# Blocks 2 to 5 take the product with w_in by quarters, with partial sums kept in one PSUM bank per pair of tiles

## The chip, the cores and the metric

One Trainium2 chip, one of its cores. The metric is the device time in microseconds (us) of one execution of the whole program. The kernel before took 990.42 us (median of three executions, 988.54 to 991.31).

## The reference

```python
for t in range(S):                                   # 4 batches, 8 heads, S = 768, head_dim 64
    state = gamma * state + k[t] (x) v[t]
    y[t]  = scale * q[t] @ state
x   = y as (3072, 512)
xn  = x / rms(x) * rms_g
x2  = (silu(xn @ w_gate) * (xn @ w_val)) @ w_out     # d_ff 1536
h   = x2 @ w_in                                      # 512 -> 1024
e   = exp(h - max(h)); solu = h * e / (sum(e) + 1e-9)
out = layernorm(solu) * g_ln @ w_out2                # 1024 -> 512
```

Everything is float32.

## The kernel before

The 3072 tokens are six blocks of 512 (`NB = 6`), each of four tiles of 128. A block goes through two stages. The first (`bc_block`, or `seven_block` for block 5) makes x2, transposed, in the four PSUM banks X0 to X3 (`XB`, a bank for 128 of the 512 features): twelve steps `m`, each with the gate product in bank GB, the value product in VB (`gv`) and their product with a slice of `w_out` (`cmm`). The second (`de_block`) takes x2 from the X banks, multiplies by `w_in`, makes softmax and layer norm, transposes and multiplies by `w_out2`. Banks SB and YB serve the attention part of the next block, which runs beside the first stage.

Every matmul of full precision is three fp32r matmuls: each operand is split into a high part (ScalarE's copy, L98) and a low part (a subtraction on VectorE or GpSimd, L99), and `mm3` (L723 to 726) multiplies high by high, high by low and low by high. `seven_block` already does the gate and value products with seven products of quarters in place of eight, with sums of the weights that `sums_steps` makes in blocks 2 to 4 and stores in DRAM.

In `de_block`, `x2_split` splits the four X banks; `d_mm(n, t, s)` makes h for tile t in two banks (`HB`): 4 slices of features x 2 halves of `w_in` x 3 matmuls, 512 columns each, and then the softmax: two maxima (L928), two exponentials (L931), two products with h (L936), and the mean taken off, one half on VectorE and one on GpSimd (L941). `t_tr(t)` transposes the result on TensorE (L951) and splits it; `e_mm(n, t, s)` multiplies by `w_out2` into one bank and sends the result out (L989, L990).

The order is d0 d1 t0 d2 t1 e0 d3 t2 e1 t3 e2 e3. Work of the next block hangs on numbered slots, called as the stages go on: `w_load` (weights from DRAM, L653, on SP's queue into the four `w4` and two `wo` buffers), the steps of the norm (`rms_steps`) and the split of the next block's normalised input into `xnh` and `xnl`. The program order gives priorities; a planner at build time orders each engine's list by them and by the times that it expects, and `issue_after` ties an instruction behind another on its engine. On the chip each engine takes its list in order.

Of the kernel before, what the change touches and what calls it, by code (L numbers as in the profile page):

```python
# [33 lines left out]
CHAIN = 12  # L34
W2_AT = [36 + 2 * j for j in range(16)]
SEVEN = (5,)
SUMS_AT = [(n, s) for n in (2, 3, 4) for s in ((3, 10, 17, 24) if n == 2 else (1, 8, 15, 22))]


@with_exitstack  # L40
def retention_moe_kernel(ctx: ExitStack, tc: tile.TileContext, qk0, q2, kt, kv, wpk, w2i, w2o,
# [512 lines left out]
    def sums_steps(j, part):  # L554
# [32 lines left out]

        return [load, none, whole, sums, none, none, parts, none, store]

    def load64(key):  # L590
# [56 lines left out]
    def w_load(g, part):  # L647
        m = g % NM
        if g < NM:
            load64((m, part))  # L650
        elif g < NG:
            w = wtile(part)
            nc.sync.dma_start(w.bitcast(F32), scr[m][part])  # L653
            wsp[g, part] = w

    def w_conv(g, part):
# [207 lines left out]
    def seven_block(n):  # L864
        base = n * NM
        for j in range(NM // 2):
# [44 lines left out]
    def d_mm(n, t, s):  # L911
# [4 lines left out]
        for i, (k, hf) in enumerate(order):  # L916
            cs = slice(hf * 512, hf * 512 + 512)
            mm3(H[hf], x2h[k][:, ts_], x2l[k][:, ts_], w2["h"][:, k, cs], w2["l"][:, k, cs],
                k == 0, k == NK - 1)
            if i == 3:  # L920
                slot(n, s)
        V = nc.vector
# [3 lines left out]
        e, u = f4(), f4()  # L926
        for hf in range(2):
            V.tensor_reduce(out=mx[:, hf:hf + 1], in_=H[hf], axis=AX.X, op=ALU.max)  # L928
        V.tensor_reduce(out=nmx, in_=mx, axis=AX.X, op=ALU.max, negate=True)
        for hf in range(2):  # L930
            nc.scalar.activation(e[:, hf, :], H[hf], AF.Exp, bias=nmx, accum_out=se[:, hf:hf + 1])  # L931
        if t == NCB - 1 and n not in (1, NB - 1) and PRE & 1:

            nc.scalar.activation(sm[:, 11:12], se[:, 1:2], AF.Silu)
        for hf in range(2):
            V.scalar_tensor_tensor(out=u[:, hf, :], in0=H[hf], scalar=1.0, in1=e[:, hf, :],  # L936
                                   op0=ALU.mult, op1=ALU.mult, accum_out=su[:, hf:hf + 1])
        V.tensor_tensor(out=mu, in0=su[:, 0:1], in1=su[:, 1:2], op=ALU.add)
        V.tensor_scalar(mu, mu, 1.0 / D_FF2, None, ALU.mult)  # L939
        for hf, eng in ((0, V), (1, nc.gpsimd)):  # L940
            eng.tensor_scalar(u[:, hf, :], u[:, hf, :], mu, None, ALU.subtract)  # L941
        lnst[t] = (u, sm)
        slot(n, s + 1)

    def t_tr(t):

        u, sm = lnst[t]
        res = []
        for b in range(2):
            bank = HB[t][b]  # L950
# [14 lines left out]
        G.tensor_tensor(out=w, in0=w, in1=r, op=ALU.mult)  # L965
        lnst[t] = (res, w)

    def e_mm(n, t, s):
        res, w = lnst.pop(t)
        r0 = n * 512 + t * P  # L970
        if n == NB - 1 and t == NCB - 1 and TAIL:

            for B, hs in ((EB[t], slice(0, 256)), (EB[0], slice(256, 512))):
# [8 lines left out]
        for f in range(NF):  # L982
            hi, lo = res[f // 4]
            cs = slice((f % 4) * P, (f % 4) * P + P)
            mm3(EB[t], hi[:, cs], lo[:, cs], w2["oh"][:, f, :], w2["ol"][:, f, :], f == 0, f == NF - 1)
            if f == 3:
                slot(n, s)
        o = f4()[:, 0, :]
        nc.scalar.mul(o, EB[t], w)  # L989
        nc.scalar.dma_start(out[r0:r0 + P, :], o)  # L990
        slot(n, s + 1)

# [15 lines left out]
    def x2_load():  # L1008
        srcs = []
        for d in range(NK):  # L1010
            t = st()
            nc.sync.dma_start(t, x2scr[d])
            srcs.append(t)
        return srcs

    def de_block(n, srcs, base):

# [130 lines left out]
    for n in range(NB):  # L1148
        if n + 1 < NB:
# [2 lines left out]
            elif n == 1:  # L1152
                begin, span, r = 35, 21, (57, 58, 59, 59, 60, 60, 61, 62, 63, 64)
            else:
                begin, span, r = 0, 28, (30, 31, 32, 32, 33, 33, 36, 38, 40, 42)
            pieces = att_pieces(n + 1)
            for i, f in enumerate(pieces):
                extra.setdefault((n, begin + i * span // (len(pieces) - 1)), []).append(f)
            if n + 1 in SEVEN:
                r = (30, 31, 32, 32, 33, 33, 36, 37, 38, 39, 40, 41, 42, 43, 44, 45, 46)  # L1160
                first7 = [lambda: seven_load(n + 1)] \
                    + [lambda i=i: w_load((n + 1) * NM + i, 2) for i in range(2)] + [seven_pump]
                for s, f in zip((37, 38, 38, 45), first7):
# [87 lines left out]
```

## Time and profile before

| | us |
|---|---|
| median of three executions | 990.42 |
| profiled execution | 990.47 |
| its span | 988.7 |
| TensorE (PE) busy | 976.0 (99%) |
| VectorE (DVE) busy | 462.8 (47%) |
| GpSimd (POOL) busy | 422.2 (43%) |
| ScalarE (ACT) busy | 395.5 (40%) |

The span runs from the first to the last instruction; what lies around it, 1.8 us, is part of the time. Busy time of TensorE includes matmuls that overlap the next one, so the distance between starts has to be read from the timeline. HBM reads were 172.05 MB and writes 38.80 MB.

### The profile page before, as it was taken

Reading aid. Unit: us, or ns where it says so; the run is one execution under the profiler, and the core shown is the slowest. Engines: PE = TensorE matmul, PEld = TensorE weight load, DVE = VectorE, ACT = ScalarE, POOL = GpSimd, SP = SyncE. Lnnn points to the kernel's source line nnn. Section 1 sums busy time; section 2 is a strip of 40 time slices with the busy share of each in tenths; the row PEclk is TensorE's granted clock in tenths of the full one; section 3 lists DMA queues with packets and bytes.
Section 4 is the critical chain, followed back from the end, with each engine's and each line's share of the span. In section 5 each row is a group of like instructions: output and inputs, shape, how many; then the busy total and the mean of one; then the engine's idle time right before and its main releaser. Section 6 shows DMA issues by size and latency. Waiting matters only on the chain.

```text
span 988.7 us, 15957 instructions
## 1 busy us (share of the span) xinstructions
PE 976.0 (99%) x5916; PEld 813.7 (82%) x5916; DVE 462.8 (47%) x920; ACT 395.5 (40%) x768; POOL 422.2 (43%) x517
## 2 busy tenths in 40 slices
PE   8999999999999999999999999999999999999998
PEld 7878787888888887888888888788888888999887
DVE  4787784662464743234462224463323353443552
ACT  4766664582344442222443123344212344221333
POOL 6876873671142593253543223655032372000031
PEclk9799999999999999999999999999999999999999
DMA  9699999887512135898523889723597724697200
GB/s 351 238 333 403 334 315 379 328 303 243 172 53 87 44 120 180 291 324 278 172 75 104 288 282 295 232 66 107 174 342 269 264 81 150 204 311 262 75 12 32
DMA packets 91021, 211.90 MB, mean 214 GB/s; under 512 B 10432, under 2 KB 36416, under 8 KB 90944
## 3 DMA queue, kind: packets, MB, share of 16 engines
q1 hardware_dynamic: 82160, 185.71, 56.1%
q10 hardware_dynamic: 8784, 25.17, 6.6%
q8 instruction: 47, 0.77, 0.3%
q14 instruction: 30, 0.25, 0.1%
HBM read 172.05 MB, written 38.80 MB: 213 GB/s over the span
## 4 chain that ended last, share of the span: by engine, by line
PE 87%; DMA 5%; POOL 3%; ACT 1%; DVE 1%; issue 1%; SPq 1%; ACTq 0%; POOLq 0%; DVEq 0%
PE X L724 12%; PE X L726 12%; PE X L725 12%; PE GB L724 7%; PE GB L726 7%; PE GB L725 7%; PE VB L724 6%; PE VB L726 6%; PE VB L725 6%; PE SB L117 3%; PE YB L117 2%; PE VB L834 2%; PE YB L834 2%; DMA x<-in_wpk 2%; PE SB L834 1%; PE GB L834 1%
## 5 line engine op out<-in xcount | busy, mean ns | idle before, releaser
L743 DVE TENSOR_TENSOR f<-VB,f 128x512 f32<-128x512 f32 x60 | 41.4, 690 | 153.6 <-PE VB L726 146.3
L725 PE MATMUL X<-r,wo 128*128 128x512 f32 x264 | 103.4, 392 | 0.0
L726 PE MATMUL X<-r,wo 128*128 128x512 f32 x264 | 103.0, 390 | 0.0
L724 PE MATMUL X<-r,wo 128*128 128x512 f32 x264 | 101.3, 394 | 0.7 <-DMA wo<-scr 0.7
L98 ACT CAST r<-f 128x512 fp32r<-128x512 f32 x72 | 44.5, 619 | 125.6 <-DVE f L743 107.8
L772 ACT ACTIVATE f<-GB 128x512 f32<-128x512 f32 x60 | 35.7, 594 | 147.7 <-PE GB L726 145.0
L625 POOL TENSOR_TENSOR st<-st,x 128x512 int32<-128x512 int32 x52 | 69.7, 1344 | 49.4 <-DVE st L624 11.3
L724 PE MATMUL GB<-xnh,w 128*128 128x512 f32 (+1 forms) x220 | 86.6, 394 | 1.7 <-ACT xnh L98 0.8
L724 PE MATMUL VB<-xnh,w 128*128 128x512 f32 (+1 forms) x220 | 86.0, 391 | 0.0
L725 PE MATMUL GB<-xnl,w 128*128 128x512 f32 (+1 forms) x220 | 85.6, 389 | 0.3 <-DVE xnl L99 0.2
L726 PE MATMUL VB<-xnh,w 128*128 128x512 f32 (+1 forms) x220 | 85.6, 389 | 0.0
L725 PE MATMUL VB<-xnl,w 128*128 128x512 f32 (+1 forms) x220 | 85.5, 388 | 0.0
L726 PE MATMUL GB<-xnh,w 128*128 128x512 f32 (+1 forms) x220 | 85.4, 388 | 0.0
L99 DVE TENSOR_TENSOR r<-f,r 128x512 fp32r<-128x512 f32 x72 | 60.4, 840 | 31.5 <-ACT r L98 31.0
L565 POOL TENSOR_TENSOR x<-x 128x512 f32<-128x512 f32 x24 | 31.0, 1292 | 98.2 <-DMA x<-scr 78.6
L961 POOL TENSOR_TENSOR sm<-sm 128x1 f32<-128x1 f32 x24 | 5.1, 214 | 134.2 <-DVE sm L939 114.7
L724 PEld LDWEIGHTS X<-r,wo 128*128 128x128 f32 x264 | 49.5, 188 | 11.4 <-issue 1.1
L726 PEld LDWEIGHTS X<-r,wo 128*128 128x128 f32 x264 | 49.6, 188 | 10.3
L725 PEld LDWEIGHTS X<-r,wo 128*128 128x128 f32 x264 | 49.6, 188 | 10.1 <-issue 0.2
L724 PE MATMUL X<-w2oh,r 128*128 128x512 f32 (+1 forms) x144 | 56.6, 393 | 0.0
L726 PE MATMUL X<-w2oh,r 128*128 128x512 f32 (+1 forms) x144 | 55.7, 387 | 0.0
L725 PE MATMUL X<-w2ol,r 128*128 128x512 f32 (+1 forms) x144 | 55.3, 384 | 0.0
(367 smaller groups left out, 2419.0 us busy)
## 6 DMA issues: line engine op xcount, KB each, us to landing
w<-scr SPq DMA_DIRECT2D x96, 512.0 KB, 4.7
wo<-scr SPq DMA_DIRECT2D x60, 512.0 KB, 4.4
x<-in_wpk SPq DMA_DIRECT2D x36, 512.0 KB, 6.2
x<-scr SPq DMA_DIRECT2D x24, 512.0 KB, 5.7
sscr<-x SPq DMA_DIRECT2D x24, 512.0 KB, 7.5
scr<-CV ACTq DMA_DIRECT2D x18, 512.0 KB, 6.1
rv<-in_kv SPq DMA_DIRECT2D x24, 256.0 KB, 4.7
scr<-w ACTq DMA_DIRECT2D x12, 512.0 KB, 5.6
```

Of the source, the lines that this page charges most:

```text
L98: h = nc.scalar.copy(hi, src)
L99: (lo_eng or nc.vector).tensor_tensor(out=lo, in0=src, in1=hi.bitcast(F32), op=ALU.subtract)
L117: return lambda: nc.tensor.matmul(out, lhsT=lhsT, rhs=rhs, start=start, stop=stop)
L565: nc.gpsimd.tensor_tensor(out=w[:, 0, :], in0=w[:, 0, :], in1=w[:, 1, :], op=ALU.add)
L625: nc.gpsimd.tensor_tensor(out=ti, in0=ti, in1=lo, op=ALU.add)
L724: nc.tensor.matmul(ps, lhsT=lh, rhs=rh, start=start, stop=False)
L725: nc.tensor.matmul(ps, lhsT=lh, rhs=rl, start=False, stop=False)
L726: return nc.tensor.matmul(ps, lhsT=ll, rhs=rh, start=False, stop=stop)
L743: recent["dve"] = nc.vector.tensor_tensor(out=a, in0=GV[1], in1=silu[:, 0, :], op=ALU.mult)
L772: recent["act"] = nc.scalar.activation(s[:, 0, :], GV[0], AF.Silu)
L834: nc.tensor.matmul(ps, lhsT=x, rhs=y[:, k, :], start=start and k + i == 0, stop=k == 1 and i == 2, skip_group_check=True)
L961: G.tensor_tensor(out=w, in0=r, in1=r, op=ALU.mult)
```

## The change

In blocks 2 to 5 `de_quarters` takes the place of `de_block`. x2 of the block is taken as quarters (tokens 0-255 and 256-511 by features 0-255 and 256-511) and `w_in` as quarters (features by halves of its 1024 columns). Seven products of quarters (`p1` to `p7`, each of two token tiles, 6 matmuls a tile) give h, with sums S1 to S4 of quarters of x2 made on VectorE and sums T1 to T4 of quarters of `w_in`. The latter are made once, in block 2 (`w2_sums`); T4 replaces a quarter of `w_in` in SBUF, T1, T2 and T3 go to DRAM and are loaded in every block, T1 into two `w4` buffers, T2 and T3 over `xnh` and `xnl`. P1, P6, P7 and, for a tile of the second pair, P4 are added up in one bank (GB for tiles 0 and 2, VB for 1 and 3); between them ScalarE copies the bank out (`keep`), and VectorE adds what P2, P5 and P3 left in X banks (`add`).

Since `xnh` and `xnl` are taken, the next block's split comes later (slots 46 to 49 in place of 36 to 42), and so do the sums of block 5's input; the first weights of blocks 3 and 4 are loaded at slots 39, 47 and 48. The sums for `seven_block` are made in two steps in block 2 and five each in blocks 3 and 4, where it was four in each. `soft` is the softmax of `d_mm`, with its tiles as arguments.

```diff
-SUMS_AT = [(n, s) for n in (2, 3, 4) for s in ((3, 10, 17, 24) if n == 2 else (1, 8, 15, 22))]
+SUMS_AT = [(2, 17), (2, 24)] + [(n, 1 + 6 * i) for n in (3, 4) for i in range(5)]
+W2_SUMS_AT = (2, 9)
+FIRST7 = 2
...
+    def w2_sums(k):
+        def whole():
+            for r in (k, k + 2):
+                W.append(wt("x2", [P, 2, 512], F32, 4))
+                nc.gpsimd.tensor_tensor(out=W[-1].rearrange("p a x -> p (a x)"), in0=w2["h"].bitcast(F32)[:, r, :],
+                                        in1=w2["l"].bitcast(F32)[:, r, :], op=ALU.add)
+        def sums():
+            (b11, b12), (b21, b22) = ((w[:, 0, :], w[:, 1, :]) for w in W)
+            for out, a, b in ((b11, b12, b11), (b12, b22, b12), (b22, b22, b11), (b21, b21, b22)):
+                nc.gpsimd.tensor_tensor(out=out, in0=a, in1=b, op=ALU.subtract)
...
-                elif g // NM not in SEVEN:
+                elif g // NM not in SEVEN and (part == 2 or g % NM > 1 or g // NM <= FIRST7):
...
@@ in bc_block @@
+        if n >= FIRST7:
+            t_load(1, n), t_load(2, n)
         cmm(n * NM + NM - 1, NM - 1)
...
@@ in seven_block @@
+        t_load(0, n)
+        with tc.issue_after(recent["wo"].ins):
+            t_load(1, n), t_load(2, n)
         out(NM - 2)
         out(NM - 1)
...
+    def t_load(i, n):
+        if i:
+            nc.sync.dma_start((None, xnh, xnl)[i].bitcast(F32), t2scr[i].rearrange("p a k x -> p (a k) x"))
+            return
+        T1[:] = [wt("w4", [P, 2, 512], F32R, 4) for _ in range(2)]
+        for a in range(2):
+            nc.sync.dma_start(T1[a].bitcast(F32), t2scr[0][:, a])
+
+    def de_quarters(n, base):
+        a11 = wt("x2", [P, 2, 2, 256], F32R, 4)
+        xh, xl = (wt("x2", [P, 2, 512], F32R, 4) for _ in range(2))
+        s3, s1, s2 = two(st()), two(st()), two(st())
+        for k in range(2):
+            split(a11[:, 0, k, :], a11[:, 1, k, :], XB[k][:, lo])
+            S.copy(s1[:, k, :], XB[k][:, hi])
+        for k in range(2):
+            V.tensor_tensor(out=s3[:, k, :], in0=XB[k][:, lo], in1=s1[:, k, :], op=ALU.subtract)
+        for k in range(2):
+            split(xh[:, k, :], xl[:, k, :], XB[2 + k])
+        for k in range(2):
+            i = V.tensor_tensor(out=s2[:, k, :], in0=XB[2 + k][:, hi], in1=s3[:, k, :], op=ALU.subtract)
+        S2 = two(r2()), two(r2())
+        s2h = S.copy(S2[0], s2)
+        s2l = V.tensor_tensor(out=S2[1], in0=s2, in1=S2[0].bitcast(F32), op=ALU.subtract)
+        S3 = parts(s3, nc.gpsimd)
...
+        def mul(bank, t, A, B, start=False):
+            ts_ = slice(t * P, t * P + P)
+            for k in range(2):
+                for i, (x, y) in enumerate(((A[0], B[0]), (A[0], B[1]), (A[1], B[0]))):
+                    nc.tensor.matmul(bank, lhsT=x[:, k, ts_], rhs=y[:, k, :], start=start and k + i == 0,
+                                     stop=k == 1 and i == 2, skip_group_check=True)
+        def keep(out, bank):
+            with tc.high_priority():
+                last["act"] = S.copy(out, bank)
+        def add(out, bank, q):
+            with tc.high_priority():
+                last["dve"] = V.tensor_tensor(out=out, in0=bank, in1=q, op=ALU.add)
...
+        def p1(t, Z):
+            mul(Z, t, A11, B11, True)
+            u[t] = f4()
+            keep(u[t][:, 0, :], Z), step()
+        def p2(t, Y):
+            mul(Y, t, A12, B21, True), add(u[t][:, 0, :], Y, u[t][:, 0, :]), step()
+        def p6(t, Z):
+            mul(Z, t, S2, T2), keep(u[t][:, 1, :], Z), step()
+        def p7(t, Z, tile):
+            mul(Z, t, S3, T3)
+            u[2 + t] = tile
+            keep(tile[:, 1, :], Z), step()
+        def p5(t, W):
+            mul(W, t, S1, (T1[0], T1[1]), True), step()
+        def c22(t, W):
+            add(u[2 + t][:, 1, :], W, u[2 + t][:, 1, :])
+        def p4(t, Z):
+            mul(Z, t, A22, T4), step()
+        def p3(t, W):
+            mul(W, t, S4, B22), add(u[t][:, 1, :], W, u[t][:, 1, :]), step()
+        p1(0, GB)
+        with tc.issue_after(s2h.ins):
+            p1(1, VB)
+        with tc.issue_after(s2l.ins):
+            p2(0, X0)
+        p6(0, GB)
+        p5(0, X1)
+        p7(0, GB, f4())
+        c22(0, X1)
+        p6(1, VB)
+        p4(0, GB)
+        soft(n, 2, (GB, u[2][:, 1, :]), halves(e2()), u[2], False)
+        p3(0, X1)
+        p7(1, VB, e2())
+        p5(1, X3)
+        with tc.issue_after(recent["sub"].ins):
+            c22(1, X3)
+        with tc.issue_after(last["act"].ins), tc.issue_after(last["dve"].ins):
+            soft(n, 0, (u[0][:, 0, :], u[0][:, 1, :]), (st(), st()), u[0], False)
+        p2(1, X2)
+        t_tr(2, (X0, X1))
+        p4(1, VB)
+        soft(n, 3, (VB, u[3][:, 1, :]), halves(e2()), u[3], False)
+        p3(1, X3)
+        soft(n, 1, (u[1][:, 0, :], u[1][:, 1, :]), halves(e2()), u[1], True)
+        t_tr(0, (X0, X1))
+        e_mm(n, 2, base + 15, GB)
+        t_tr(3, (X0, X1))
+        e_mm(n, 0, base + 17, X2)
+        t_tr(1, (X0, X1))
+        e_mm(n, 3, base + 19, X3)
+        e_mm(n, 1, base + 21, X2, True)
...
-        de_block(n, XB, 35)
+        if n >= FIRST7:
+            de_quarters(n, 35)
+            continue
+        de_block(n, XB, 35)
```

## Rows read from the trace of the kernel before

**Rows 1.** The page: busy us, share of the span, instructions of each engine.
```profile
PE 976.0 (99%) x5916; PEld 813.7 (82%) x5916; DVE 462.8 (47%) x920; ACT 395.5 (40%) x768; POOL 422.2 (43%) x517
```

**Rows 2.** Windows of stages: busy us of each engine, granted clock, DMA share, GB/s.
```profile
385.00:481.00 96.00, 96.00 (x621) 78.73 (x618) 32.48 (x58) 28.19 (x56) 41.15 (x48) 1.00 0.84 281
481.00:537.00 56.00, 56.00 (x352) 45.67 (x352) 26.36 (x69) 23.28 (x52) 25.51 (x44) 1.00 0.28 89
...
841.00:937.40 96.40, 95.73 (x651) 88.53 (x650) 40.86 (x94) 24.02 (x46) 1.15 (x4) 1.00 0.67 219
```

**Rows 3.** Waits of TensorE: us in total, times, longest us.
```profile
PE GB L724 <- ACT xnh L98: 0.8, 1, 0.8
...
PE X L724 <- DMA wo<-scr: 0.7, 1, 0.7
```

**Rows 4.** Tile x, TensorE's instructions: duration ns min/median/max, first and last start.
```profile
L724 PE MATMUL X<-w2ih,x x120: 389/389/496, 269.4 to 966.1; 128*128 128x512 f32 x120
...
L724 PE MATMUL VB<-w2ih,x x48: 389/389/497, 262.1 to 963.4; 128*128 128x512 f32 x48
```

**Rows 5.** TensorE's timeline in block 2: start us, duration us, instruction.
```profile
474.57 0.39 PE L726 MATMUL VB<-xnh,w 128*128 128x512 f32 x1
...
481.29 0.39 PE L724 MATMUL GB<-w2ih,x 128*128 128x512 f32 x1
...
489.29 0.39 PE L724 MATMUL X<-w2ih,x 128*128 128x512 f32 x1
...
494.50 0.39 PE L726 MATMUL X<-w2ih,x 128*128 128x512 f32 x1
...
508.20 0.39 PE L726 MATMUL GB<-w2oh,r 128*128 128x512 f32 x1
...
513.64 0.40 PE L726 MATMUL X<-w2ih,x 128*128 128x512 f32 x1
```

**Rows 6.** ScalarE's timeline in block 2, idle time before in brackets.
```profile
479.44 2.64 ACT L98 CAST x<-X 128x512 fp32r<-128x512 f32 x4 [0.94 <-PE X L726]
...
508.71 0.69 ACT L989 ACTIVATE f<-GB,sm 128x512 f32<-128x512 f32 x1 [2.71 <-PE GB L726]
```

**Rows 7.** VectorE's timeline in block 2.
```profile
480.48 2.48 DVE L99 TENSOR_TENSOR x<-X,x 128x512 fp32r<-128x512 f32 x4
...
488.81 0.69 DVE L928 TENSOR_REDUCE sm<-GB 128x1 f32<-128x512 f32 x1
...
493.60 0.49 DVE L941 TENSOR_SCALAR f<-f,sm 128x512 f32<-128x512 f32 x1
```

**Rows 8.** GpSimd's timeline in block 2.
```profile
493.70 1.83 POOL L941 TENSOR_SCALAR f<-f,sm 128x512 f32<-128x512 f32 x1
...
521.86 1.56 POOL L941 TENSOR_SCALAR f<-f,sm 128x512 f32<-128x512 f32 x1
```

**Rows 9.** Lines L743 (page: busy, mean ns), L772 and L860 (min/median/max).
```profile
L743 DVE TENSOR_TENSOR f<-VB,f 128x512 f32<-128x512 f32 x60 | 41.4, 690 | 153.6 <-PE VB L726 146.3
...
L772 ACT ACTIVATE f<-GB x60: 573/597/600, 42.4 to 788.9; 128x512 f32<-128x512 f32 x60
...
L860 DVE TENSOR_TENSOR f<-VB,st x6: 424/425/425, 852.7 to 926.4; 128x256 f32<-128x256 f32 x6
```

**Rows 10.** DMA issues: KB each, median us from issue to landing.
```profile
w<-scr SPq DMA_DIRECT2D x96, 512.0 KB, 4.7
```

**Rows 11.** GpSimd's timeline, sums of block 5's input, first and last of 11.
```profile
793.57 3.80 POOL L99 TENSOR_TENSOR xnl<-xT,xnh 128x512 fp32r<-128x512 f32 x3 [0.73 <-ACT xnh L98]
...
806.19 1.30 POOL L99 TENSOR_TENSOR qd<-xT,qd 128x512 fp32r<-128x512 f32 x1
```

**Rows 12.** TensorE's timeline in block 5, first and last of the stretch.
```profile
937.42 0.39 PE L724 MATMUL GB<-w2ih,x 128*128 128x512 f32 x1
...
985.05 0.28 PE L726 MATMUL GB<-w2oh,r 128*128 128x256 f32 x1
```

**Rows 13.** Window in the start-up, columns as in rows 2.
```profile
30.00:45.00 15.00, 14.00 (x97) 12.58 (x97) 11.91 (x16) 9.97 (x18) 14.46 (x18) 0.66 0.56 190
```

More of the change, by code (lines that the diff above doesn't have):

```diff
@@ L588, in sums_steps, with tied, parts, parts2 @@
         return [load, none, whole, sums, none, none, parts, none, store]
+    t2scr = [dp.tile([P, 2, 2, 512], F32, tag=f"t2scr{i}", name=f"t2scr{i}") for i in range(3)]
+    def w2_sums(k):
+        W, o = [], []
+        def whole():
[7 more added lines that the diff above has]
+                nc.gpsimd.tensor_tensor(out=out, in0=a, in1=b, op=ALU.subtract)
+        def tied(hi, lo, t):
+            with tc.issue_after(recent["act"].ins), tc.issue_after(recent["dve"].ins):
+                split(hi, lo, t)
+        def parts():
+            for t in (W[0][:, 0, :], W[1][:, 1, :]):
+                o.append(wt("x2", [P, 2, 512], F32R, 4))
+                tied(o[-1][:, 0, :], o[-1][:, 1, :], t)
+        def parts2():
+            tied(w2["h"][:, k, 512:], w2["l"][:, k, 512:], W[1][:, 0, :])
+            h, l = (wt("st", [P, 512], F32R, 3) for _ in range(2))
+            tied(h, l, W[0][:, 1, :])
+            o.extend((h, l))
+        def store():
+            for i in range(2):
+                nc.sync.dma_start(t2scr[i][:, :, k, :], o[i].bitcast(F32))
+        def store2():
+            for i in range(2):
+                nc.sync.dma_start(t2scr[2][:, i, k, :], o[2 + i].bitcast(F32))
+        def none():
+            pass
+        return [whole, none, sums, none, parts, parts2, store, store2]
     def load64(key):
@@ L652, in w_load @@
             w = wtile(part)
-            nc.sync.dma_start(w.bitcast(F32), scr[m][part])
+            recent["wo"] = nc.sync.dma_start(w.bitcast(F32), scr[m][part])
             wsp[g, part] = w
@@ L921, in d_mm, with halves, soft @@
                 slot(n, s)
+        soft(n, t, H, halves(f4()), f4(), t == NCB - 1)
+        slot(n, s + 1)
+    def halves(t):
+        return t[:, 0, :], t[:, 1, :]
+    def soft(n, t, H, e, u, final):
         V = nc.vector
@@ L925, in d_mm @@
         nmx, mu = sm[:, 6:7], sm[:, 7:8]
-        e, u = f4(), f4()
         for hf in range(2):
@@ L930, in d_mm @@
         for hf in range(2):
-            nc.scalar.activation(e[:, hf, :], H[hf], AF.Exp, bias=nmx, accum_out=se[:, hf:hf + 1])
-        if t == NCB - 1 and n not in (1, NB - 1) and PRE & 1:
+            nc.scalar.activation(e[hf], H[hf], AF.Exp, bias=nmx, accum_out=se[:, hf:hf + 1])
+        if final and n not in (1, NB - 1) and PRE & 1:
             nc.scalar.activation(sm[:, 11:12], se[:, 1:2], AF.Silu)
         for hf in range(2):
-            V.scalar_tensor_tensor(out=u[:, hf, :], in0=H[hf], scalar=1.0, in1=e[:, hf, :],
+            V.scalar_tensor_tensor(out=u[:, hf, :], in0=H[hf], scalar=1.0, in1=e[hf],
                                    op0=ALU.mult, op1=ALU.mult, accum_out=su[:, hf:hf + 1])
@@ L940, in d_mm, with t_tr @@
         for hf, eng in ((0, V), (1, nc.gpsimd)):
-            eng.tensor_scalar(u[:, hf, :], u[:, hf, :], mu, None, ALU.subtract)
+            i = eng.tensor_scalar(u[:, hf, :], u[:, hf, :], mu, None, ALU.subtract)
+            if eng is V:
+                recent["sub"] = i
         lnst[t] = (u, sm)
-        slot(n, s + 1)
-    def t_tr(t):
+    def t_tr(t, banks=None):
         u, sm = lnst[t]
@@ L949, in t_tr @@
         for b in range(2):
-            bank = HB[t][b]
+            bank = (banks or HB[t])[b]
             run([lambda j=j: nc.tensor.transpose(bank[:, j * P:j * P + P], u[:, b, j * P:j * P + P], ident)
@@ L966, in t_tr, with e_mm @@
         lnst[t] = (res, w)
-    def e_mm(n, t, s):
+    def e_mm(n, t, s, bank=None, final=False):
         res, w = lnst.pop(t)
+        bank = bank or EB[t]
         r0 = n * 512 + t * P
-        if n == NB - 1 and t == NCB - 1 and TAIL:
-            for B, hs in ((EB[t], slice(0, 256)), (EB[0], slice(256, 512))):
+        if n == NB - 1 and final and TAIL:
+            for B, hs in ((bank, slice(0, 256)), (GV[0], slice(256, 512))):
                 for f in range(NF):
@@ L984, in e_mm @@
             cs = slice((f % 4) * P, (f % 4) * P + P)
-            mm3(EB[t], hi[:, cs], lo[:, cs], w2["oh"][:, f, :], w2["ol"][:, f, :], f == 0, f == NF - 1)
+            mm3(bank, hi[:, cs], lo[:, cs], w2["oh"][:, f, :], w2["ol"][:, f, :], f == 0, f == NF - 1)
             if f == 3:
@@ L988, in e_mm @@
         o = f4()[:, 0, :]
-        nc.scalar.mul(o, EB[t], w)
+        nc.scalar.mul(o, bank, w)
         nc.scalar.dma_start(out[r0:r0 + P, :], o)
@@ L1154, in retention_moe_kernel @@
             else:
-                begin, span, r = 0, 28, (30, 31, 32, 32, 33, 33, 36, 38, 40, 42)
+                begin, span, r = 0, 28, (30, 31, 32, 32, 33, 33, 46, 47, 48, 49)
+                extra.setdefault((n, 31), []).append(lambda n=n: t_load(0, n))
+                if n + 1 not in SEVEN:
+                    for s, i, part in ((39, 0, 0), (39, 0, 1), (47, 1, 0), (48, 1, 1)):
+                        extra.setdefault((n, s), []).append(
+                            lambda g=(n + 1) * NM + i, part=part: w_load(g, part))
             pieces = att_pieces(n + 1)
@@ L1166, in retention_moe_kernel @@
                 extra.setdefault((n, s), []).append(f)
+            if n == 2:
+                for k in range(2):
+                    for i, f in enumerate(w2_sums(k)):
+                        extra.setdefault((n, W2_SUMS_AT[k] + i), []).append(f)
             for i, (b, s) in enumerate(SUMS_AT):
```

35 lines of the change are left out of this document (33 added, 2 removed).

## The prediction

> **What bounds the kernel now.** I read the busy times first: TensorE is busy 976.0 of 988.7 us [rows 1]. That is an average, so the stages come next: in the projection stretch of block 2 and the stretch ahead of it TensorE is busy for every microsecond, at full granted clock, while VectorE, ScalarE and GpSimd stand at 42 to 47% in the first and DMA falls from 0.84 to 0.28 [rows 2]. Then TensorE's waits: outside the start-up the longest are 0.7 and 0.8 us, once each [rows 3]. So the end is set by how many matmuls there are and how far apart they start. The busy duration of one (0.39 us) is no price: they are pipelined. In the timeline the 24 matmuls of one token tile start at 489.29 to 494.50, (494.50-489.29)/23 = 0.2265 us apart [rows 5]. That is the price of a 512-wide matmul here.
>
> **The change part by part.** The sum is made against the profiled execution, 990.47 us (span 988.7), which stands 0.05 us above the median of 990.42.
>
> *Matmuls removed.* x @ w_in takes 4 tiles x 4 k x 2 halves x 3 = 96 matmuls a block, 576 in six blocks; a third of these (192) come from L724, of which the rows show 120 on X banks and 48 on VB, the other 24 being on GB [rows 4]. By quarters it is 7 products x 2 tiles x 2 k x 3 = 84. Blocks 2 to 5 lose 4 x 12 = 48, all of the same shape: 48 x 0.2265 = 10.87 us, all on the path. Transposes, the product with w_out and everything in the gate and value stages stay. Without any new wait: 990.47 - 10.87 = 979.6.
>
> *Sums of x at the start of each product stretch.* Let T be the first matmul of the stretch (481.29 in block 2) [rows 5]; one product on one tile takes 6 x 0.2265 = 1.36 us. Today ScalarE takes the four X banks from 479.44 to 482.08 and VectorE follows to 482.96 [rows 6, 7]. New are, ahead of S2, four half-wide subtractions on VectorE (0.42 us, as L860 [rows 9]) and two half-wide copies on ScalarE. VectorE's list (six half-wide at 0.42, two full at 0.69, 3.9 us) ends between 483.3, if the starts overlap as today (2.48 us for four of 0.69), and 484.4. S2's halves then cost 0.6 and 0.69: ready between 484.6 and 485.7. Due: the fourth product, T+4.08 = 485.4, its third matmul at 485.8. I take 0.3 us lost a block; ends 0 and 0.5. S1, S3 and S4 are due later, at T+5.4, T+6.8 and T+10.9, and the first two also fit; S3 and S4 take their low halves on GpSimd (1.30 us [rows 11]).
>
> *Partial sums in one bank.* GB takes P1, P6, P7 and P4 of a tile in turn, and between them ScalarE copies it. A result is readable 0.51 us after its last matmul's start (508.20 to 508.71) [rows 5, 6], the copy costs 0.59 [rows 9]: 5 x 0.2265 + 0.51 + 0.59 = 2.23 us from a product's start until the bank is free. Exactly one other product stands between at the tightest places (P6 to P7, P7 to P4), so it is due after 2.72: 0.49 us to spare, if ScalarE is free. VB has more between. I take 0.1 us a block; ends 0 and 1.2 (these two links, each late by one other 0.6 us instruction). Behind a late matmul the whole queue of TensorE waits, as it is in order. The six VectorE additions (0.69 us [rows 9]) are needed by the softmax or by P3 on X1 and X3, which comes at least 1 us later; nothing for these alone.
>
> *Softmax and transposes.* Today a whole tile's product (5.4 us) and more lies between softmaxes; now C for tile 2 is complete at T+11.2 (eight products and 0.3), and the next three tiles follow within 9 us. One softmax took from 488.81 to 494.09 on VectorE's half and 495.53 on GpSimd's [rows 7, 8], the slowest to 523.42, 9.4 us after its last matmul had ended (513.64+0.4, GpSimd was busy with other sums) [rows 5, 8]. The transposes of tile 2 are due after 12 products, T+16.3, and its two halves come at about T+15.9 and T+17.2; P4 of tile 1 can go between. I take 0.3 us a block; ends 0 and 1. The last tile: VectorE does per tile two reductions, two multiplications, a subtraction, small ones, two splits and about one addition. With starts 0.61 to 0.67 apart that is 5.5 us, 9.4 at worst; I take 5.9. The last e_mm may start at T+11.2+4x5.9+1.8 (GpSimd's half)+2.7 (transposes, copy, split) = T+39.3. TensorE gets there by itself at 14 x 1.36 + 4 x 0.9 (8 transposes each) + 3 x 5.44 = T+39.0. So 0.3 us are lost in block 5, where nothing follows. In blocks 2 to 4 the next block's gate matmuls (24, 5.4 us) can be put ahead, and cover it.
>
> *T1, T2, T3 from DRAM.* 3 MB more a block on SP's queue. T1 takes two w4 buffers free two steps earlier. T2 and T3 take xnh and xnl, which the last value matmul frees at 474.57+0.4 = 475.0 [rows 5]; due at T+4.08 = 485.4 and T+6.8 = 488.1. A 512 KB load lands after 4.7 us [rows 10]; at the rate of the stage before (281 GB/s at a share of 0.84, so 335 [rows 2]) 512 KB take 1.6 us, so 3.1 are fixed: an estimate of 475.5+3.1+6.3 = 484.9 for both. It hides, with 3 us to spare; at the other end, four loads of 4.7 one behind the other, T3 lands at 493.8 and 5.7 us a block are lost. On SP the next block's first weights stand behind these loads; they are due 30 us later.
>
> *Moved work.* The next block's x halves are now split only when T2 and T3 are used, T+14, rather than beside the last product; they have 30 us. For block 5 the eleven operations of its sums took GpSimd from 793.57 to 807.49 [rows 11], 13.9 us; from T+14 they end near T+36 with softmax work between: hidden, cover about 8 us. The extra sums of w_in in block 2 (some 21 us of GpSimd) replace two of the four sums steps there; GpSimd was busy 41 of 96 us [rows 2]. A fifth sums step in blocks 3 and 4 adds 2 MB to some 27. Nothing for all these; if DMA has no room left, two weight waits of 0.7 us a block, as in [rows 3].
>
> *Sum.* Lost: blocks 2 to 4 0.3+0.1+0.3 = 0.7 each, block 5 1.0, together 3.1. 979.6 + 3.1 = **982.7**.
>
> **Rivals.** *The bank links hold TensorE.* Copy and product alternate with 0.49 us to spare; ScalarE has 0.6 to 1.0 us instructions of the softmax and of the attention of the next block in the same stretch. Both links late by 0.6 and S2 by 0.5: 1.7 a block, 7 in all, and with the 3.1 less what they share about 989. Against it: today TensorE waits nowhere here for a copy. The Trainium skill speaks for it (PSUM — Partial Sum Buffer, section on bank collisions): two engines may not touch one bank in the same quadrant at once, so that each copy needs a semaphore on both sides. The trace agrees, as the copy of GB begins only after its last matmul has ended [rows 5, 6]; a stop at each link is this rival.
>
> *Slower: the softmaxes become a chain.* Four softmaxes on VectorE, ScalarE and GpSimd within a stretch of TensorE that is 2.7 us shorter and puts its products first. With p us a tile, block 5 loses 4p-23.3 and blocks 2 to 4 about 2 less each (5.4 of cover against 3.5 of attention work on VectorE). The gain is gone at p = 6.7; at 7 the time is 979.6+2.8+13 = 995. For it: the slow case of 9.4 us [rows 5, 8]. Against it: VectorE is at 47% in this stretch [rows 2], and the 9.4 included a wait for GpSimd.
>
> *T2 or T3 late.* If 2 MB of other loads run beside them, T3 lands at about 491, 3 us late in each block: 979.6+3.1+12 = 995. Against: DMA share of 0.28 in this stretch.
>
> *The clock falls.* In the start-up stretch from 30 to 45 us, where TensorE was busy 14.0 of 15 us, the granted clock was 0.66 [rows 13], so part of it was at 1.2 GHz. Products at that level would cost 84 x 0.2265 = 19 us more a block, 1059 in all. The Trainium skill (TensorE: Matmul & The Clock Gate, section on a second HAM failure mode) tells of a kernel that cycles through PSUM banks with short idle times between groups, and whose clock went up and down; by that, new short waits would be enough. This trace speaks against it: the stretch from 841 to 937, with 0.7 us of waits, stayed at 1.00 [rows 2].
>
> **How the numbers follow.** Forecast 0.62 (its own range 979.8 to 986), bank links 0.18 (986 to 991), softmax chain 0.12 (991 to 1005), late T3 0.06, clock 0.02. About 0.3% (3 us) can be told from no change. Faster: 0.61 and half of the bank links, 0.70. Same: the other half, and the mild ends of the next two, 0.14. Slower: 0.16. The range 979.6 to 991.0 leaves out some 0.18, nearly all above.
>
> **What would show it.** Right: 5868 matmuls (48 fewer), starts still 0.2265 apart, TensorE's waits below 1 us a block. The S2 step: a wait of the fourth product for ScalarE or VectorE. The bank links: waits of matmuls on GB or VB for the copy. The softmax: waits of transposes, longest in block 5; its stretch from first product to last matmul was 937.42 to 985.05 [rows 12], 47.6 us, and should be near 46. T2, T3: waits on DMA. The prediction is wrong if the waits add up to over 8 us, or if the gate stages of blocks 3 and 4 begin to wait for weights.

## The result, and the profile after

The changed kernel takes 1000.62 us in the median (998.94 to 1004.74) beside 989.55 us for the kernel before on the same chip: a ratio of 1.0116, 95% interval 1.0081 to 1.0151. It is slower by 11 us, outside the range of 979.6 to 991.0, where 982.7 was forecast. The 10.87 us of matmuls did go; 22 us came in their place.

The page of the changed kernel, busy times (answers to [rows 1]):
```profile
PE 966.0 (97%) x5868; PEld 800.6 (80%) x5868; DVE 506.4 (51%) x992; ACT 422.5 (42%) x824; POOL 455.6 (46%) x537
```
5868 matmuls are 48 fewer, and TensorE is busy 10.0 us less, yet the span is 997.2 us. So it waits, and the view of its waits from 380 us on, where the kernel before has one of 0.7 us, says for what (us in total, times, longest):
```profile
PE X L1010 <- DVE f L999: 4.9, 4, 1.7
PE SB L119 <- DVE A L262: 4.1, 2, 2.0
PE VB L1136 <- ACT x L1145: 2.7, 3, 0.9
PE YB L119 <- ACT sq L321: 2.5, 2, 1.2
PE GB L773 <- DVE sm L987: 1.9, 2, 1.0
PE X L771 <- DMA wo<-scr: 1.2, 1, 1.2
PE SB L883 <- POOL xnl L101: 0.9, 1, 0.9
PE X L1010 <- DVE r L101: 0.4, 1, 0.4
```
Together 18.6 us. Only one of the waits is for a load; 16.5 us are for VectorE and ScalarE. A wait costs more than its row says, as TensorE's timeline in block 5 shows:
```profile
958.23 0.39 PE L1136 MATMUL X<-w2ih,r 128*128 128x512 f32 x1
959.52 0.50 PE L1136 MATMUL VB<-w2ih,x 128*128 128x512 f32 x1 [0.90 <-ACT x L1145]
959.86 0.40 PE L1136 MATMUL VB<-w2il,x 128*128 128x512 f32 x1
```
The matmul that waited 0.90 us starts 1.06 us later than 0.2265 us after the one before it, which is 0.16 us more, and the next one starts 0.34 us behind it in place of 0.2265. With 0.16 to 0.27 us more for each, the 16 waits cost 21 to 23 us, an estimate from this one wait.

Cut at the first product matmul of blocks 2 to 5 and at the last matmul, one profiled execution each, us:

| kernel | block 2 to 3 | 3 to 4 | 4 to 5 | 5 to end |
|---|---|---|---|---|
| before | 157.97 | 158.27 | 139.89 | 47.63 |
| after | 160.83 | 159.79 | 142.89 | 51.38 |
| e1 | 157.81 | 157.36 | 146.50 | 50.33 |
| e3 | 157.98 | 158.41 | 142.86 | 48.43 |
| e11 | 161.33 | 161.34 | 146.71 | 52.45 |
| e13 | 158.09 | 158.19 | 144.37 | 48.07 |
| e12 | 158.21 | 156.86 | 141.98 | 45.79 |

With quarters and no new wait each would be 2.72 shorter than before (12 x 0.2265). The change adds 11.13 in all, so 22.0 are lost: 5.6, 4.2, 5.7 and 6.5. The waits are nearly all of it. (e1 to e13 are the experiments below.) Ahead of block 2 the profiled execution of the changed kernel (after) is 2.66 us shorter, 2.2 of it already at 260 us, in work that both share (granted clock 0.94 against 0.91 in the first 60 us); that is not the change's.

The window of the product stretch of block 2, columns as in [rows 2]:
```profile
496.00:521.00 25.00, 19.81 (x174) 15.35 (x173) 23.90 (x68) 17.14 (x40) 17.92 (x24) 1.00 0.37 112
```
VectorE is busy 23.9 of 25 us. In the kernel before it is busy 16.75 us in the fullest of seven such windows between 478 and 535 us (485 to 510), and 47% over the whole stretch [rows 2]. It looks like a full engine. What it does with that time, in block 5 of after, is the reading that the rest hangs on (VectorE's timeline; VB and x hold the two halves of tile 3's sums, f those of the other tiles):
```profile
961.33 0.49 DVE L999 TENSOR_SCALAR f<-f,sm 128x512 f32<-128x512 f32 x1
...
962.33 1.27 DVE L986 TENSOR_REDUCE sm<-f 128x1 f32<-128x512 f32 x2
963.52 0.68 DVE L986 TENSOR_REDUCE sm<-VB 128x1 f32<-128x512 f32 x1
964.11 0.68 DVE L986 TENSOR_REDUCE sm<-f 128x1 f32<-128x512 f32 x1
964.71 0.68 DVE L986 TENSOR_REDUCE sm<-x 128x1 f32<-128x512 f32 x1
965.30 0.68 DVE L101 TENSOR_TENSOR r<-X,r 128x512 fp32r<-128x512 f32 x1
...
971.43 0.69 DVE L994 SCALAR_TENSOR_TENSOR f<-f,x 128x512 f32<-128x512 f32 x1
...
972.12 0.83 DVE L999 TENSOR_SCALAR f<-f,sm 128x512 f32<-128x512 f32 x1
...
973.20 0.64 DVE L999 TENSOR_SCALAR x<-x,sm 128x512 f32<-128x512 f32 x1
...
973.93 0.90 DVE L999 TENSOR_SCALAR f<-f,sm 128x512 f32<-128x512 f32 x1
```
L999 ends a softmax. Tile 2's ends at 961.33. Then the maxima of tiles 0, 3 and 1 stand side by side, then their products, and all three end within 1.8 us, tile 0, which TensorE wants first, 10.8 us after tile 2. Tile 2's split (965.30) stands behind other tiles' maxima as well. Taken by the mean VectorE is faster than the 5.9 us a tile of the prediction, (973.93-961.33)/3 = 4.2 us; it finishes three things late instead of one early.

### The profile page after: what moved, and what is told of

It is laid out like the page before. It is cut to its first block, busy times and chain, and to the rows that moved or that the text cites. A ratio compares the mean times of both kernels' runs of the same rounds, so it can differ in the third digit from the quotient of the medians.

```text
span 997.2 us, 16099 instructions
## 1 busy us (share of the span) xinstructions
PE 966.0 (97%) x5868; PEld 800.6 (80%) x5868; DVE 506.4 (51%) x992; ACT 422.5 (42%) x824; POOL 455.6 (46%) x537
## 4 chain that ended last, share of the span: by engine, by line
PE 84%; DVE 6%; DMA 5%; ACT 2%; POOL 2%; issue 1%; SPq 0%; ACTq 0%; POOLq 0%
PE X L771 10%; PE X L773 10%; PE X L772 10%; PE GB L773 6%; PE GB L771 6%; PE GB L772 6%; PE VB L771 5%; PE VB L773 5%; PE VB L772 5%; PE SB L119 3%; PE GB L1136 2%; PE X L1136 2%; PE VB L883 2%; PE YB L883 2%; PE VB L1136 2%; DMA x<-in_wpk 2%
## 5 line engine op out<-in xcount | busy, mean ns | idle before, releaser
L772 PE MATMUL X<-r,wo 128*128 128x512 f32 x264 | 103.2, 391 | 0.0
L672 POOL TENSOR_TENSOR st<-st,x 128x512 int32<-128x512 int32 x52 | 70.0, 1349 | 47.7 <-DVE st L671 11.2
L772 PE MATMUL GB<-xnl,w 128*128 128x512 f32 (+1 forms) x220 | 85.0, 386 | 0.3 <-DVE xnl L101 0.2
L772 PE MATMUL VB<-xnl,w 128*128 128x512 f32 (+1 forms) x220 | 85.0, 386 | 0.0
L101 POOL TENSOR_TENSOR r<-st,r 128x512 fp32r<-128x512 f32 x8 | 10.3, 1293 | 115.7 <-ACT r L100 113.9
L772 PEld LDWEIGHTS X<-r,wo 128*128 128x128 f32 x264 | 49.6, 188 | 10.1 <-issue 0.2
L772 PE MATMUL X<-w2ol,r 128*128 128x512 f32 (+1 forms) x144 | 55.7, 387 | 0.0
```

The lines of the kernel that those rows point to most:

```text
L101: (lo_eng or nc.vector).tensor_tensor(out=lo, in0=src, in1=hi.bitcast(F32), op=ALU.subtract)
L672: nc.gpsimd.tensor_tensor(out=ti, in0=ti, in1=lo, op=ALU.add)
L772: nc.tensor.matmul(ps, lhsT=lh, rhs=rl, start=False, stop=False)
```

## Experiments

Theories. A, amount: VectorE has too much to do in the stretch. B, order: the lists of VectorE and ScalarE, which each engine works off in turn, hold the first-needed softmax behind the others. C: the copy that frees VB stands behind an exponential in ScalarE's list. The gains below are differences of medians; the runs stem from several chips, on which the kernel before took 989.6 to 990.4 us, and small differences between versions, up to some 4 us beside the changed kernel with its wide interval, are not clear of noise.

**e1 and e2, amount.** The three maxima a tile go, in the changed kernel (e1) and in the one before (e2).
```
-        for hf in range(2):
-            V.tensor_reduce(out=mx[:, hf:hf + 1], in_=H[hf], ...op=ALU.max)
-        V.tensor_reduce(out=nmx, in_=mx, ..., negate=True)
-   nc.scalar.activation(e[hf], H[hf], AF.Exp, bias=nmx, accum_out=...)
+   nc.scalar.activation(e[hf], H[hf], AF.Exp, accum_out=...)
```


> The changed kernel, with the subtraction of the row maximum ahead of the exponential left out (two maxima and their combination per tile; the quotient is the same up to rounding). VectorE loses about 1.45 us a tile, 5.8 us a block. Theory A (VectorE is full for some 25 us of each product stretch and TensorE waits for what comes last there): most of the 22 us of waits go, 982 to 990 us. Theory B (the planner's order, which takes the softmaxes of three tiles in turn, makes the first one late): half of it at most, 992 to 997. Theory C (a copy of a PSUM bank stands behind an exponential in ScalarE's list): the three waits of 0.9 us, 997 to 998.

> The kernel before, with the same maxima left out. There TensorE has no waits in these stretches, so all theories expect no change: 988 to 991 us. If it gains as much as the changed kernel does, the gain has nothing to do with the change.

e1 998.78 us, ratio 1.0088 (1.0059 to 1.0116); e2 989.15, 0.998 (0.9966 to 0.9994). Some 5.7 us a block taken off VectorE (4 x (1.27 + 0.15)) gained 1.8 in all. The intervals of e1 and of the changed kernel overlap, and e2 gains 0.2% by the same cut, so this is no gain that could be put down to the change. Three stretches got shorter, block 4's grew, mostly by one wait (TensorE's timeline of e1, then VectorE's):
```profile
821.85 0.78 PE L773 MATMUL GB<-w2oh,r 128*128 128x512 f32 x1 [4.49 <-DVE sm L993]
822.43 0.63 PE L771 MATMUL GB<-w2oh,r 128*128 128x512 f32 x1
822.85 0.63 PE L772 MATMUL GB<-w2ol,r 128*128 128x512 f32 x1
```
```profile
816.68 1.04 DVE L991 SCALAR_TENSOR_TENSOR f<-f,x 128x512 f32<-128x512 f32 x1
...
817.66 1.74 DVE L991 SCALAR_TENSOR_TENSOR x<-x,x 128x512 f32<-128x512 f32 x1
...
821.12 0.68 DVE L101 TENSOR_TENSOR r<-X,r 128x512 fp32r<-128x512 f32 x1
```
The matmul needed the split of tile 2 (821.12); the products of three other tiles stood ahead of it, two of which took 1.04 and 1.74 us in place of 0.69. TensorE's clock fell behind this wait and behind one of 2.05 us in block 5, which by the granted clock cost e1 some 3.4 us more (last section). Less work, worse order: A alone falls.

**e3, order.** Tile 3's softmax is tied behind tile 0's subtraction, tile 1's behind tile 3's; no work changes.
```
+        with tc.issue_after(recent["sub"].ins):
             soft(n, 3, ...)
...
+        with tc.issue_after(recent["sub"].ins):
             soft(n, 1, ...)
```


> The changed kernel, with VectorE's part of the softmax of tile 3 tied behind the last subtraction of tile 0, and tile 1's behind tile 3's: same work, taken one tile after the other. Theory B: tile 0 is ready some 4 us earlier, the transposes' waits (1.0, 1.5, 0.7 and 1.7 us) go and with them 4 to 8 us: 993 to 997. Theory A: VectorE's work is the same, and gaps come in while it waits for ScalarE; no gain, 999 to 1004. Theory C: no change.

994.63 us, ratio 1.0045 (1.0021 to 1.0069): 6.0 us back. VectorE's timeline in block 5 of e3:
```profile
958.87 0.49 DVE L999 TENSOR_SCALAR f<-f,sm 128x512 f32<-128x512 f32 x1
...
965.17 0.49 DVE L999 TENSOR_SCALAR f<-f,sm 128x512 f32<-128x512 f32 x1
...
967.88 0.69 DVE L994 SCALAR_TENSOR_TENSOR x<-VB,x 128x512 f32<-128x512 f32 x1 [0.84 <-ACT x L989]
...
970.30 0.49 DVE L999 TENSOR_SCALAR x<-x,sm 128x512 f32<-128x512 f32 x1
```
Tile 0 ends 6.3 us after tile 2 instead of 10.8, although VectorE now even idles (0.84 us for an exponential).

**e4, filler.** The next block's attention matmuls, which the planner puts into the product stretch of blocks 2 and 3, are tied behind the next gate product.
```
+    def held(f):
+        with tc.issue_after(recent["gv"].ins):
+            f()
...
+            if n > 2:
+                pieces = [lambda f=f: held(f) for f in pieces]
```


> The changed kernel, with the matmuls of the next block's attention tied behind the first gate product of blocks 3 and 4, so that they can't be put into the product stretches of blocks 2 and 3. VectorE then has some 5 us less there. Theory A: the waits for the attention's operands (6.6 us in blocks 2 and 3) go, and some of the transposes' waits: 993 to 996. Theory B: the 6.6 us go and the rest stays, 994. Theory C: no change but for them. If the attention work is only a filler, TensorE waits for the transposes in its place: 999 to 1002.

1004.49 us, 1.0135 (1.011 to 1.016): 3.9 us above the changed kernel by the median, though the intervals overlap; no gain at any rate. The waits for attention operands are gone, but new ones stand ahead of the gate stage (1.31 us at 538.22, 1.32 at 700.86) and of block 3's product with S2 (0.66 at 647.37), and the stretch has lost matmuls that it could do meanwhile. So the attention there covered at least as much as it cost.

**e5 and e6, the copy of VB.** Tile 2's softmax is written behind the last sum in VB, and its exponentials are tied behind that copy (e5); the same with e3's ties (e6).
```
-        soft(n, 2, (GB, u[2][:, 1, :]), ...)
         p3(0, X1)
         p7(1, VB, e2())
+        with tc.issue_after(last["act"].ins):
+            soft(n, 2, (GB, u[2][:, 1, :]), ...)
```


> The changed kernel, with the softmax of tile 2 written behind P3 of tile 0 and P7 of tile 1, and its exponentials tied behind ScalarE's copy of VB: the copy no longer stands behind an exponential that waits for a maximum. Theory C (this copy holds P4 of tile 1): the waits of 0.9 us in blocks 2, 3 and 5 go, and TensorE gains up to 1.06 us each: 997 us. Theory B (order of the softmaxes on VectorE): TensorE only arrives earlier at the next wait, and tile 0 is as late as before: 999 to 1001.

> Both: softmaxes of tiles 0, 3 and 1 one after the other, and the copy ahead of the exponentials. If both causes stand by themselves, about 3 us below the serial version: 991 to 992. If the copy's wait is only passed on to the transposes of tile 2, as the serial version: 994 to 995. Theory A (VectorE full): no better than the serial version.

e5 997.6, 1.0069 (1.0049 to 1.009); e6 995.26, 1.0057 (1.0036 to 1.0078). The waits of 0.90 us are gone, so C is right about them, but tile 2's exponentials come later and its transposes wait 1.71, 1.71, 2.72 and 1.5 us in both. e5's gain of 3.0 us is not clear of noise, and on top of e3 (e6) there is none: the wait is passed on. In e6's profiled execution, the slowest of its five, TensorE's clock fell twice behind these waits.

**e7, amount and order.** e6 without the maxima.

> Both, and the subtraction of the row maximum left out as well (the quotient is the same up to rounding). With the order mended, the two maxima are part of each tile's chain (1.45 us of 5.5). Theory B: the waits for the transposes of tile 2 (1.5 and 0.7 us) go too: 986 to 989, below the kernel before. Theory A: as much or more, 983 to 986. If something else holds TensorE (attention, DMA, block 5's sums on GpSimd): 990 to 992.

989.84 us, 1.0003 (0.9988 to 1.0018): with the list in order, the same cut that gave 1.8 us in e1 gives 5.4 against e6, clear of noise. So amount counts, once order lets it. Part of the 5.4 may be the clock: it falls nowhere in e7's product stretches, and twice in those of e6.

**e8, place.** Quarters in block 5 only; the others multiply as before, but from block 2's sums on a quarter of w_in holds T4, so that blocks 2 to 4 compute with other numbers.
```
-FIRST7 = 2
+FIRST7 = 5
...
```
The lines that are left out put the split of the next block's input back to the slots of the kernel before.

> Blocks 2 to 4 as before (product with w_in whole), block 5 alone by quarters; the sums of w_in are still made in block 2. In the profiles the stretch from block 5's first product to its last matmul grew from 47.6 to 51.4 us, with no attention work and hardly any DMA beside it. If that is the product stretch's own order and copies (theories B and C): 3 to 4 us above the kernel before, 993 to 995, and each of the other blocks adds 1.5 to 3. If it came from the blocks ahead of it (late weights, late sums): no change, 989 to 991.

993.38 us, 1.0022 (1.0008 to 1.0036). The stretches of blocks 2 to 4 are within 0.14 us of the kernel before; block 5 to the end takes 52.65 us, 5.0 more than before, with the waits of after (0.90, 0.70, 1.00, 1.69). It is 1.3 us longer than in after; here the clock fell behind the last of them (granted 0.63 and 0.52 in the windows from 968 to 972 us). So block 5's loss belongs to its own product stretch and not to the blocks ahead; for the other blocks this was not tried.

**e9 and e10, transposes later.** e6 and e7 with the transposes of tile 2 tied behind the last product, and their splits given priority.
```
         p3(1, X3)
+        with tc.issue_after(last["mm"].ins):
+            t_tr(2, (X0, X1))
```


> As e6 (softmaxes one behind the other, copies of VB ahead of the exponentials), with the transposes of tile 2 tied behind the last product (1.36 us later), and the splits behind all transposes of these blocks given priority in the planner's list, so that tile 2's split no longer stands behind other tiles' products on VectorE. Order theory: e6 lost about 1.7, 1.7, 2.7 and 1.5 us to waits of tile 2's transposes and 0.6 to 1.3 three times behind them; the later place covers 1.36 us of each, so about 5 of 995.3 go and the time is 988 to 992. Capacity theory (VectorE's list is full, any reordering only passes the wait on): 994 to 997, with the waits now at the first product with w_out of tile 2.

> e9 without the row maximum of the softmax (the exponential is taken of the sums as they are), three reductions fewer on VectorE a tile in blocks of both kinds. Both reliefs together: from e7 (989.8) the same 1.36 us a block go, so 984 to 987, of which 0.4 is what the kernel before gains from the same cut (989.15). Capacity theory: order is worth nothing beyond e7, 989 to 991. If it comes below 987, the 10.87 us of removed matmuls do show once VectorE's list is both shorter and in the order of need; if it stays near 990, something else than the lists of VectorE and ScalarE holds the product stretch.

1001.58, 1.0118 (1.0101 to 1.0136), and 995.02, 1.0046 (1.0029 to 1.0064): both slower than e6 and e7, a miss. The last product takes X3, which an addition frees that is tied behind tile 2's subtraction; TensorE, with nothing left to go first, waited up to 3.33 us for it.

**e11 and e13, order again.** That addition gets priority instead of the tie, on top of e3 (e11). It turned out that this tie had also kept tile 0 behind tile 2; e13 puts that back and has e11's instructions in another order.
```
-        with tc.issue_after(recent["sub"].ins):
+        with tc.high_priority():
             c22(1, X3)
# e13 besides:
-        with tc.issue_after(last["act"].ins), tc.issue_after(last["dve"].ins):
+        with tc.issue_after(recent["sub"].ins):
             soft(n, 0, ...)
```


> As e3 (softmaxes one behind the other), but the addition that frees X3 (into the partial sum of tile 3) is no longer tied behind tile 2's subtraction: it has priority and stands in VectorE's list between tile 2's two products. So TensorE can take the last product (P3 of tile 1, 1.36 us) before the transposes of tile 2. In e9 it was this tie that held the last product for 2.2 to 3.3 us in two blocks. Order theory: the transposes of tile 2 are covered by 1.36 us more, tile 2's softmax comes 0.69 us later: 0.5 to 0.7 us a block better than e3's 994.6, so 991.5 to 993.5, transposes of tile 2 waiting under 1.5 us. Capacity theory: the same as e3 within 1 us. If it is over 996, the addition ahead of tile 2's softmax costs more than the cover gives.

> e11 with one tie more: tile 0's softmax behind tile 2's subtraction (the tie that the early addition had taken away without replacing it), so that all four softmaxes stand one behind the other in VectorE's list. Same instructions as e11, another order. Order theory: e11's 1009.0 came from tile 0's two reductions standing between tile 2's two products; with the tie it returns to 992.5 to 995.5. Capacity theory: nothing changes in the work, so 1005 to 1012. A rival for e11, that the early addition itself costs: over 1000.

e11 1009.01, 1.0198 (1.0181 to 1.0215); e13 994.69, 1.0039 (1.0021 to 1.0056). VectorE's timeline in block 2 of e11, then of e13:
```profile
499.75 0.68 DVE L994 SCALAR_TENSOR_TENSOR f<-GB,x 128x512 f32<-128x512 f32 x1
...
500.96 1.27 DVE L986 TENSOR_REDUCE sm<-f 128x1 f32<-128x512 f32 x2
502.15 0.68 DVE L994 SCALAR_TENSOR_TENSOR f<-f,x 128x512 f32<-128x512 f32 x1
...
505.32 0.48 DVE L999 TENSOR_SCALAR f<-f,sm 128x512 f32<-128x512 f32 x1
```
```profile
499.77 0.68 DVE L994 SCALAR_TENSOR_TENSOR f<-GB,x 128x512 f32<-128x512 f32 x1
...
500.98 0.68 DVE L994 SCALAR_TENSOR_TENSOR f<-f,x 128x512 f32<-128x512 f32 x1
...
502.09 0.49 DVE L999 TENSOR_SCALAR f<-f,sm 128x512 f32<-128x512 f32 x1
...
502.49 1.27 DVE L986 TENSOR_REDUCE sm<-f 128x1 f32<-128x512 f32 x2
```
Up to 500.96 the two are the same. In e11 two maxima of tile 0 and then other work slip in; tile 2's subtraction ends 3.2 us later, and TensorE waits there for 2.01 and 1.30 us instead of 0.77. The same instructions, 14.3 us apart by order: B is shown. But the 14.3 are not the waits alone. In e11 the clock fell behind such waits in all four blocks and in e13 in none; by the granted clock of windows around them e11 lost 1.7, 1.7, 1.7 and 3.4 us to it, 8.5 of the 13.1 us by which the stretches of the two differ.

**e12 and e14, all together.** e7 with the early addition (e12), and with e13's tie too (e14).

> e7 (softmaxes in turn, copies of VB ahead of the exponentials, no row maximum) with the same early addition; leaves out the row maximum in all blocks. Order theory: e7 waited 1.42, 1.42 and 1.22 us for the transposes of tile 2 in blocks 2 to 4; most of that goes behind the last product, so 986 to 988. Capacity theory: 989 to 991, as e7 (989.84). If it is slower than e7, the order in which the planner now puts tile 2's splits behind other tiles' products costs more than the cover gives.

> e12 with the same tie (tile 0's softmax behind tile 2's subtraction): copies of VB first, all softmaxes in turn, early addition; leaves out the row maximum in all blocks. Order theory: tile 2's subtraction no longer has a product of tile 0 ahead of it (0.6 us) and its split comes 0.6 us earlier: 0.5 us a block better than e12's 988.1, so 985.5 to 988. Capacity theory: the same as e12 within 0.6 us. Against the kernel before without the maximum (989.15) a time under 987 would be the first in which the removed matmuls show.

e12 988.09, 0.9984 (0.9971 to 0.9997); e14 990.58, 1.0003 (0.999 to 1.0016). e12 stands beside 989.15 for the kernel before with the same cut, whose interval it overlaps: no gain from quarters. What e12 still loses is waits as well, eleven from block 2 on with 7.8 us together. e14's tie, harmless with the maxima, pushed a split of block 4 behind other products (one wait of 4.11 us). No version with the maxima beat the kernel before.

## Why the prediction was wrong

*Matmuls removed* was right: 48 fewer, starts still 0.2265 us apart, busy 10.0 us less.

*Sums of x* was right: no matmul waits for S2, against 0.3 us a block. In block 5 S2 was ready at T+3.8 (945.93), ahead of T+4.08. The early bound of its sum is off: 3.9 us of work from 480.48 with starts that overlap as quoted end at 483.7 to 484.0, not 483.3; nothing hung on it.

*T1, T2, T3 from DRAM* was right: no matmul waits for them; the one wait for a load is for the weights wo (1.2 us, 0.7 before). *Moved work* was taken at nothing. It cost one wait of 0.9 us, for a low half of x that GpSimd now splits late, and probably more: the sums of block 5's input now run on GpSimd beside tile 2's softmax in block 4. VectorE's timeline there, then GpSimd's:
```profile
817.34 1.29 DVE L994 SCALAR_TENSOR_TENSOR f<-f,x 128x512 f32<-128x512 f32 x1 [0.26 <-ACT x L989]
...
818.68 1.09 DVE L996 TENSOR_TENSOR sm<-sm 128x1 f32<-128x1 f32 x1
```
```profile
816.78 2.98 POOL L437 TENSOR_TENSOR xT<-xT 128x512 f32<-128x512 f32 x2
```
The same two instructions take 0.69 and 0.15 us in block 5 (960.21, 960.95), where GpSimd is idle; in block 4 the second ends together with GpSimd's (819.77, 819.76), and tile 2's transposes wait 1.53 us instead of 0.70. No run took the sums away, so this cause is read from the trace and not shown by an experiment.

*Partial sums in one bank* was too small where it bit: 0.90 us in three blocks, and not at GB, which it named as tightest, but at VB, of which it said that there is more between; the copy stands behind an exponential that waits for a maximum. In ScalarE's timeline in block 2 of after:
```profile
497.03 0.69 ACT L989 ACTIVATE x<-GB,sm 128x512 f32<-128x512 f32 x1 [2.99 <-DVE sm L987]
...
497.71 0.58 ACT L1145 COPY x<-VB 128x512 f32<-128x512 f32 x1
```
The prediction had its condition, "if ScalarE is free", and priced a 0.6 us instruction ahead, not one that itself waits 2.99 us. But e5 and e6 show that this wait is one face of the next step's: freed, it goes on to the transposes.

*Softmax and transposes* is the step that failed: it took 0.3 us a block. Two of its terms were wrong.

The first is when tile 2's product is complete, T+11.2, after eight products as the program writes them. The planner's list for TensorE has P4 of tile 0, which completes it, as the eleventh. In block 5 of after (T = 942.14), TensorE's timeline, then VectorE's:
```profile
955.74 0.39 PE L1136 MATMUL GB<-w2ih,x 128*128 128x512 f32 x1
```
```profile
957.30 0.69 DVE L986 TENSOR_REDUCE sm<-GB 128x1 f32<-128x512 f32 x1 [3.36 <-PE GB L1136]
```
So tile 2's first maximum starts at T+15.2, after VectorE had idled 3.36 us for it; in blocks 2 and 3, where attention matmuls come in between as well, at T+17.5. Only three products are left behind it to cover the softmax. All versions with quarters have this order and none changes it, so its price is open.

The second is that softmaxes follow one another at 5.9 us of VectorE a tile, by which tile 0 is done at T+11.2+2x5.9+1.8 = T+24.8, the last 1.8 for GpSimd's half. Measured, a tile cost less, 4.2 us, but the tiles did not follow one another: the planner's list took them in turn. In block 5 VectorE's half of tile 0 began at T+30.0 and GpSimd's ended at T+31.4; that is 6.6 us late, of which 4.0 are the late start; the rest is the taking in turn less what a cheaper tile saves. In e3, one tile after the other, VectorE's half came at T+25.5. With tile 2's late split this makes the 7.2 us of waits for transposes and first products with w_out; the copy's 2.7 come on top.

The cover that it counted on, the next block's 5.4 us of gate matmuls, came too late: at 501 and 507 us in block 2, and likewise in block 3, the planner put attention, whose matmuls wait for the same two engines (4.1 and 2.5 us), and block 3's gate and value matmuls begin only at 516.24, behind the last of block 2's waits.

The rival that the softmaxes become a chain had the right sign, and its span of 991 to 1005 holds the 1000.62, with a chance of 0.12. That is luck as far as its mechanism goes: its price at 4.2 us a tile would have been nothing. The bank links did hold TensorE, at another bank and by 0.90 us where 0.6 was priced. The clock's rival did not come in the profiled execution of the changed kernel: its window stands at 1.00, and its longest wait is 2.04 us.

What order and amount are worth by themselves: order alone 6.0 us (e3 against after), amount alone 1.8, within the noise, both with the copy first 10.8 (e7), with the addition early 12.5 (e12). So the order of the softmaxes is shown for 6 of the 22 us, order and amount together, with the copy and the addition moved, for 11 to 13; the rest is waits that no version took away. Open is how the planner's estimates come to this order, what the late P4 costs, whether GpSimd's sums are why block 4 to 5 takes 2 us and more longer than before in every version with quarters there, and whether an order exists that keeps the maxima and wins. The 2.72 us less were met in no stretch; block 5 of e12 comes nearest (45.79 against 47.63, or 47.39 in e2, which lacks the maxima too).

## What to carry to other kernels

Where work is taken from the busiest engine, ask how close together the consumers' inputs now come ready: several chains that used to be apart will share one in-order list, and then the first-needed result comes as late as the last. Price the first one by what may stand ahead of it in the list, not by mean cost a tile, and tie the chains one behind the other before judging the change. Take the times at which inputs come ready from the list that the planner made, not from the program as it is written: the product that the first softmax needs stood eleventh, not eighth. A freed wait is only a gain if the next one in the list is not as late.

## What the runs showed of the hardware

A short stop can cost its clock as well. After e11's two waits in block 2 (2.01 and 1.30 us, ahead of 505.86 and 507.81) the windows show (columns as in [rows 2]):
```profile
506.00:508.00 2.00, 0.70 (x6) 0.46 (x6) 1.97 (x8) 0.59 (x1) 1.95 (x3) 1.00 0.36 104
508.00:510.00 2.00, 2.00 (x24) 1.25 (x23) 1.92 (x7) 1.49 (x3) 0.89 (x3) 0.68 0.38 111
510.00:512.00 2.00, 2.00 (x21) 1.67 (x17) 1.77 (x4) 0.55 (x4) 1.52 (x4) 0.50 0.08 20
512.00:514.00 2.00, 2.00 (x9) 1.67 (x10) 0.07 (x1) 1.94 (x6) 1.77 (x4) 0.96 0.36 132
```
0.50 is 1.2 GHz. The clock falls when TensorE is busy again, and returns some 4 us on. Over 506 to 514 the granted clock falls short by (0.32 + 0.50 + 0.04) x 2 = 1.7 us of full clock, an estimate of what the fall costs on top of the waits. In e1, after 4.49 us, matmuls start 0.43 us apart (822.43 to 822.85) instead of 0.2265. It is not the length of one wait alone: in e6 a wait of 1.71 us in block 2 (ahead of 504.28) left the clock at 1.00, and the same wait in block 3 (ahead of 662.31) was followed by 0.50; in after 2.04 us left it at 1.00. What else decides was not tried. In the profiled executions such falls stand in the product stretches of e1, e5, e6, e8, e9, e10, e11 and e14 and not in those of after, e3, e4, e7, e12 and e13, so they belong to the price of an order and are part of the differences above. The Trainium skill (TensorE: Matmul & The Clock Gate, section on a second HAM failure mode) tells of a clock that goes up and down where short idle times stand between groups of matmuls; e11 agrees, the changed kernel itself, with 16 such waits, does not.
